# In the last but one attention slot, the last weight load is issued ahead of three row stores instead of behind them

## The chip, the cores and the metric

The kernel runs on one core of a Trainium2 chip. The metric is the device time of one execution in microseconds (us), as the median of several runs. The profile is one further execution of the same program, taken by the hardware profiler. All moments below are microseconds from the start of its span.

Five engines run their own instruction queues and meet at semaphores: TensorE (PE: matmuls; PEld is its weight load), VectorE (DVE), ScalarE (ACT), GpSimd (POOL) and SyncE (SP). SP and GpSimd issue the DMAs; the page of the profile shows SP's as queue q1 (hardware) and GpSimd's as queue q0 (software).

## The reference

Blockwise causal attention, and then a mixture of eight experts, of which each token uses one:

```python
# attention: batch 8, heads 8, sequence 576, head size 64; blocks of 64 positions
scores = where(block_of(q) >= block_of(k), q @ k.T / 8, -1e9)
x = softmax(scores) @ v                      # joined over heads: [8, 576, 512]

# experts: E = 8, D = 512, F = 1024, token after token within a batch
logits = x @ w_gate                          # [8, 576, 8]
local_gate = sigmoid(x @ w_local)
e = argmax(logits[s]) if s == 0 or local_gate[s] < 0.5 else previous e
p = softmax(logits[s])
out[s] = p[e] * (relu(x[s] @ w1[e]) @ w2[e])
```

The expert of a token can depend on all tokens before it in its batch.

## The kernel before, in words

**Attention.** A pair is two heads of one batch; the eight batches have four pairs each, 32 in all (`NPAIR`). A loop over `i` has one slot for each pair. Slot `i` issues the loads of q and k of pair `i + 2` (SP), the product of pair `i - 1` with its values (`values`, lines 998 and 1007), the scores of pair `i` (`scores`, lines 972 to 977), their exponentials on ScalarE, and the transposes of q and k of pair `i + 1` (`transposes`, tile `kq`, line 692). `add_chunks` (lines 1019 and 1021) adds up the chunks of a pair's exponentials on VectorE, for their sums.

**Rows of x.** In slots of their own, the finished pairs of a batch are transposed into token rows (`rows_of_batch`, PSUM tile `trx`), and VectorE multiplies them by the softmax's reciprocals into an SBUF tile (line 818). Up to batch 5 that tile is a slice of `xg`; for the later batches it is `x`, a tile of a pool with two buffers. Slot 30 makes three such tiles of batch 6: two in `x` and one, of 64 rows, in `xg`. Slot 31 makes two more, in the two buffers of `x` again. A call to `store` only notes the transfer to the DRAM tensor `x_rows`; `release` (line 677) issues what is noted, at the end of slots 0 to 30 on GpSimd's queue, and after slot 31 on SP's.

**Weights of the experts.** They lie in SBUF in bf16, `w1_bf` and `w2_bf` (both are called `w_bf` in the profile). `load_weights(e, layer)` is one DMA from GpSimd that converts 2 MB of f32 to 1 MB of bf16: line 107 for `w1`, line 111 for `w2`. There are sixteen, one in every second slot from slot 2 on for the first fourteen. The place of the last expert's `w1` holds routing scratch until slot 30, and that of its `w2` holds q and k that are waiting for their transposes, so these two loads come last: line 107 between the first gathers (`pending`), and line 111 at the end of slot 30.

**Experts.** Tokens are sorted into tiles of 128 by expert. `gather` (line 651, GpSimd) fetches a tile's rows from `x_rows` into `xg`; SP's DMA transpose turns it (line 1269 for the first four tiles, into a part of `S`; line 1393 for the others). `first_mm` (line 1093) multiplies by the tile's `w1`, which VectorE has copied out (line 1078 for tiles 0 and 1, into `Pc` and `qkT`; line 1297 for the others, `w1c`); ScalarE applies the relu (line 1096); `second_mm` (line 1335) multiplies by `w2_bf` in place, at an offset that is read at run time; ScalarE scales `y` (line 1340) and GpSimd scatters it to the output (line 1343). Tiles of the first five batches run while batch 7 is still being routed: its logits (lines 705 and 728), and `tokens` on VectorE with small products on TensorE between (lines 313 to 395).

**Order.** The scheduler is manual: each engine takes its instructions in the order in which the program is written, and semaphores for data and for buffers' reuse are put in by the framework. The transposes, the scores, the routing's products and `first_mm` of tile 0 all take PSUM from one pool of three buffers in rotation (tag `sc`). Between slot 31 and the later experts' tiles stands `nc.gpsimd.drain()` (line 1277).

Of the kernel before, what the change touches and what calls it, by code (L numbers as in the profile page):

```python
# [62 lines left out]
def kernel(  # L63
# [23 lines left out]
    E = moe_w_gate.shape[1]  # L87
# [17 lines left out]
    def load_weights(e, layer):  # L105
        if layer == 0:
            nc.gpsimd.dma_start(
                out=w1_bf[:, e * WE:(e + 1) * WE].rearrange("p (do f) -> p do f", f=F),
                in_=moe_w1[e].rearrange("(do di) f -> di do f", di=P))
        else:  # L110
            nc.gpsimd.dma_start(
                out=w2_bf[:, e * WE:(e + 1) * WE].rearrange("p (fo d) -> p fo d", d=Dm),
                in_=moe_w2[e].rearrange("(fo fi) d -> fi fo d", fi=P))

    HP = H // 2
    NPAIR = B * HP
# [715 lines left out]
    with tc.tile_pool(name="atn_const", bufs=1) as cst, \  # L832
# [24 lines left out]
        def load_qk(i):  # L857
            if i >= NPAIR:
                return
            b, p = divmod(i, HP)  # L860
            h2 = slice(2 * p, 2 * p + 2)
            tl = ld.tile([P, 2, D], F32, tag="qkl", name="qkl")
            raws[i] = [tl]
            for j, src in enumerate((k, q)):

                m = staged_of(i)[:, j].rearrange("p (h j d) -> p h j d", h=2, j=4)
                nc.sync.dma_start(
                    out=m.rearrange("p h j d -> p h (j d)"),
                    in_=src[b, h2, :512].rearrange("h (p j) d -> p h (j d)", j=4))
                raws[i].append(m)  # L870
            for j, src in enumerate((k, q)):
                nc.sync.dma_start(out=tl[64 * j:64 * j + 64],
                                  in_=src[b, h2, 512:].rearrange("h s d -> s h d"))
# [81 lines left out]
        def scores(i, u):  # L955
            if i >= NPAIR:
                return
            if u == 0:
                Ss[i] = Sb[i % NSB]
            t = qkTs[i % 2]  # L960
            ps = psp.tile([P, 2, 512], F32, tag="sc", name="sc")
            col = 0
            for c, q0, n in UNITS[u]:
                for half in (1, 0):
                    late = half
                    skip = ST if late and q0 == c * P else 0
                    k0 = c * P + ST * late
                    for h in range(2):
                        r = slice(64 * h, 64 * h + 64)
                        to = ps[64 * half:64 * half + 64, h]  # L970
                        if skip and c == 0:
                            nc.tensor.matmul(to[:, col:col + ST], lhsT=t[r, 0, LAST:],
                                             rhs=t[r, 1, LAST:], start=True, stop=True)
                        elif skip:
                            nc.tensor.matmul(to[:, col:col + ST], lhsT=minus[r], rhs=ones_b[r, :ST],
                                             start=True, stop=True)
                        nc.tensor.matmul(to[:, col + skip:col + n], lhsT=t[r, 0, k0:k0 + ST],  # L977
                                         rhs=t[r, 1, q0 + skip:q0 + n], start=True, stop=True)
                col += n
            return ps  # L980

        def exps(i, u, ps):
            if i >= NPAIR:
                return
            for col, n, c, q0 in EXPS[u]:
                rows = slice(0, P)
                nc.scalar.activation(exps_at(i, c, q0, n, rows), ps[rows, :, col:col + n],  # L987
                                     func=AF.Exp, scale=scale_attn)
# [88 lines left out]
        def weights_at(w, ev):  # L1077
            nc.vector.tensor_copy(w, w1_bf[:, bass.ds(ev, WE)])
            return w
# [21 lines left out]
        def expert(ph, j, engines=(mybir.EngineType.PE, mybir.EngineType.DVE)):  # L1101
            return nc.values_load(
                et_i[ph][0:1, j:j + 1], engines=engines, min_val=0,
                max_val=(E - 1) * WE,
                skip_runtime_bounds_check_because="the table is clamped to the last expert")

        def bf(x, n):
            return x.rearrange("p a s -> p (a s)").bitcast(BF16)[:, :n]
# [62 lines left out]
        def behind(i):  # L1171

            def between():
                if i % HP == 2 and i < NPAIR - 2 or i == NPAIR - HP or not routing(i) and i > 1:
                    vector(AHEAD_OF[i % HP])
                run(sums)
                if sums:
                    routing(i)

            sums = sums_of(i)  # L1180
            if sums:
                values(i - 1, between)
            else:
                values(i - 1)
                between()
            if not swap:
                add_chunks(i - 1)
            if i == NPAIR - 2:
                mask(i - 1, nc.vector)
            load_v(i + 1)  # L1190
            if i > 1 and not rows_first(i):
                vector(AFTER[i % HP])
# [5 lines left out]
        for i in range(NPAIR):  # L1198
            slot[0] = i
            load_qk(i + 2)  # L1200


            swap = i == 1
            if not swap:
                behind(i)
            if i == NPAIR - 1:

                tiles = [(0, j) for j in range(NS[0])] + [(1, j) for j in range(NS[1])]
                ev = {j: expert(*tiles[j]) for j in range(2)}
                w = weights_at(bf(Pc[0], WE), ev[0])  # L1210
            for u in range(len(UNITS)):
                ps = scores(i, u)
                if u < 2 or i < 2:
                    exps(i, u, ps)
                if u == 0:
                    if i == 0:
                        transposes(1, 8)
                        constants()
                        for h in range(2):
                            hs = slice(64 * h, 64 * h + 64)  # L1220
                            nc.sync.dma_start(
                                out=wg2[hs, :, 16 * h:16 * h + E],
                                in_=moe_w_gate.rearrange("(p h d) e -> h d p e", h=2, d=D)[h])
                            nc.sync.dma_start(
                                out=wg2[hs, :, 16 * h + E:16 * h + E + 1],
                                in_=moe_w_local.rearrange("(p h d) e -> h d p e", h=2, d=D)[h])
            if swap:
                behind(i)
            last = lambda: exps(i, 2, ps) if i > 1 else None
            if i == NPAIR - 2:  # L1230
                last()
                last = lambda: None
                run([lambda: half_batch(B - 1, 0)])
            if i:
                transposes(i + 1, 6 if swap else 0,
                           last)
            if swap:
                add_chunks(i - 1)
            if i == NPAIR - 1:
                routing(i)  # L1240
            run(turns_of(i))
            if rows_first(i):
                vector(AFTER[i % HP])
            slot[0] = i + 0.5
            if i % HP == 0 or NPAIR - 3 <= i < NPAIR - 1:
                routing(i)
            if i < NPAIR - 1:
                vector(END[i % HP])
            early_mask = i % 2 == 0 and i <= NPAIR // 2
            if early_mask:  # L1250
                mask(i - 1, nc.gpsimd)
            arrange(i + 2, [nc.gpsimd.tensor_copy] * 2)
            if not early_mask and i != NPAIR - 2:
                mask(i - 1, nc.gpsimd)
            while pending:
                pending.pop(0)()

            if wload < 2 * E - 2 and i == 2 + 2 * wload:
                load_weights(*divmod(wload, 2))
                wload += 1  # L1260
            if i < NPAIR - 1:
                release(queue=nc.gpsimd)
            if i == NPAIR - 2:

                free = bf(Sb[(NPAIR - 3) % NSB], 2 * S * 2)[:, -AHEAD * Dm:]
                xTs = {}
                for j in range(AHEAD):
                    xTs[j] = free[:, j * Dm:(j + 1) * Dm].rearrange("p (k n) -> p k n", k=KO1)
                    nc.sync.dma_start(out=xTs[j], in_=row_of_x(xgs[j]), transpose=True)
                load_weights(E - 1, 1)  # L1270
        assert not pending
        slot[0] = NPAIR
        release()
# [17 lines left out]
    with ExitStack() as ffn:  # L1291
# [184 lines left out]
        i = len(tiles) - 1  # L1476
# [37 lines left out]
```

## Time and profile before

| What | Value |
|---|---|
| Time, median of 3 runs | 408.97 us (408.6 to 411.11) |
| Time of the profiled execution | 408.54 us |
| Its span | 406.5 us |
| PE busy | 392.6 us |
| DVE, ACT, POOL busy | 242.2, 228.7, 196.1 us |
| Queue q0 (GpSimd's DMAs) | 34.84 MB, 41.6% of 16 engines' span |
| Queue q1 (SP's DMAs) | 34.19 MB, 37.2% |
| Loads of weights | 16, 1024 KB each, median 9.9 us from issue to landing |

A row of a timeline reads: start, duration, engine, line, operation, what is written `<-` what is read, shapes, count; in brackets the engine's idle time before it and what ended that. A row of the DMA view reads: transfer, issuing queue, count, size of one, and the median time from issue to landing, where the profile has it.

### The profile page before, as it was taken

How to read it: one execution, taken by the hardware profiler on the slowest of the kernel's cores; microseconds unless marked ns; L12 is line 12 of the kernel's file. 1: busy time of each engine (PE TensorE's matmuls, PEld its weight loads, DVE VectorE, ACT ScalarE, POOL GpSimd, SP SyncE). 2: the span in 40 equal slices, each digit the busy share in tenths (PEclk: the TensorE clock that was granted, in tenths of full speed). 3: DMA queues.
4: the chain of work that ended last, by engine and by line, in shares of the span. 5: the costliest groups of instructions: out<-in, count | busy, mean ns of one | idle time of the engine just before them, and what ended most of it. 6: DMA issues, size and time to landing. Idle time of an engine off the chain costs nothing. (4 is left out here: it accounts for less than half of the span.)

```text
span 406.5 us, 14547 instructions
## 1 busy us (share of the span) xinstructions
PE 392.6 (97%) x5834; PEld 285.5 (70%) x5834; DVE 242.2 (60%) x505; ACT 228.7 (56%) x391; POOL 196.1 (48%) x250
## 2 busy tenths in 40 slices
PE   9999999999999999999998998998999999999985
PEld 7667677677677677667766666666777777777763
DVE  2463564564564577967899975977887333333320
ACT  3758557567557557657647465333545555555542
POOL 1244251342341342582632363074776888888833
PEclk9999999999999999999999999999999999999999
DMA  6588989999999979999989689944763645655532
GB/s 178 142 190 194 216 172 222 201 201 228 194 202 210 183 183 246 174 202 244 170 192 237 136 155 192 151 109 120 166 168 97 170 135 148 154 149 149 128 99 78
DMA packets 108819, 69.97 MB, mean 172 GB/s; under 512 B 74847, under 2 KB 100255, under 8 KB 108752
## 3 DMA queue, kind: packets, MB, share of 16 engines
q0 software_dynamic: 19200, 34.84, 41.6%
q1 hardware_dynamic: 89552, 34.19, 37.2%
q8 instruction: 48, 0.79, 0.8%
q14 instruction: 19, 0.16, 0.1%
HBM read 66.88 MB, written 14.70 MB: 201 GB/s over the span
## 5 line engine op out<-in xcount | busy, mean ns | idle before, releaser
L1019 DVE TENSOR_TENSOR S<-S,Pc 128x896 f32<-128x896 f32 (+2 forms) x96 | 84.0, 875 | 23.9 <-PE o L998 19.1
L977 PE MATMUL sc<-qkT 64*64 64x224 f32 (+6 forms) x1536 | 91.6, 367 | 0.0
L1297 DVE COPY w1c<-w_bf 128x4096 bf16 x36 | 44.3, 1231 | 55.6 <-PE ps_h L1093 52.8
L1093 PEld LDWEIGHTS <-w1c 128*128 128x128 bf16 x1152 | 67.2, 98 | 9.1 <-issue 1.3
L880 POOL COPY w_bf<-w_bf 128x512 f32<-128x512 f32 x61 | 43.9, 737 | 60.8 <-DMA w_bf<-in_k_dram 33.0
L977 PEld LDWEIGHTS sc<-qkT 64*64 64x64 f32 x1536 | 70.5, 134 | 3.7 <-issue 2.5
L1335 PE MATMUL ps_y<-w_bf,hT 128*128 x296 | 69.9, 379 | 1.0 <-DMA w_bf<-in_moe_w_dram 1.0
L987 ACT ACTIVATE Pc<-sc 128x448 f32<-128x448 f32 (+1 forms) x96 | 68.1, 716 | 0.0
L1093 PE MATMUL ps_h<-xT,w1c 128*128 128x128 bf16 x1088 | 66.3, 219 | 1.3 <-ACTq L1474 1.1
L1343 POOL DMA_INDIRECT out_dram<-y,idx x37 | 56.2, 1519 | 22.0 <-ACT y L1340 12.2
L651 POOL DMA_INDIRECT xg<-x_rows,idx x38 | 47.1, 1239 | 31.3 <-issue 13.9
L1096 ACT ACTIVATE hT<-ps_h 128x512 bf16<-128x512 f32 x76 | 45.3, 597 | 26.2 <-PE ps_h L1093 24.6
L998 PE MATMUL o<-Pc,v 128*64 128x320 f32 (+2 forms) x512 | 57.3, 366 | 0.0
L998 PEld LDWEIGHTS o<-Pc,v 128*64 128x64 f32 x512 | 34.6, 137 | 24.1
L1340 ACT ACTIVATE y<-ps_y,xg 128x512 f32<-128x512 f32 x37 | 25.4, 687 | 45.5 <-PE ps_y L1335 39.1
L987 ACT ACTIVATE S<-sc 128x576 f32<-128x576 f32 x64 | 42.0, 656 | 12.6 <-PE sc L977 12.1
L1335 PEld LDWEIGHTS <-hT 128*128 128x128 bf16 x296 | 27.5, 98 | 27.3 <-issue 1.0
L1011 ACT COPY oT<-o 128x576 f32<-128x576 f32 x32 | 20.5, 641 | 35.7 <-PE o L1007 35.7
L1026 POOL MEMSET S<- 64x128 f32 x30 | 6.0, 200 | 69.8 <-DVE S L1021 40.7
L818 DVE TENSOR_TENSOR xg<-trx,rs 128x512 bf16<-128x512 f32 (+1 forms) x31 | 20.2, 685 | 25.9 <-PE trx L692 25.8
L998 PE MATMUL o<-S,v 128*64 128x192 f32 (+1 forms) x256 | 34.7, 392 | 0.3 <-ACT qkT L925 0.3
L714 ACT COPY LT<-trg 128x320 f32<-128x320 f32 x15 | 6.4, 426 | 44.4 <-PE trg L705 44.4
(313 smaller groups left out, 467.4 us busy)
## 6 DMA issues: line engine op xcount, KB each, us to landing
w_bf<-in_moe_w_dram POOLq DMA_DIRECT2D x16, 1024.0 KB, 9.9
w_bf<-in_k_dram SPq DMA_DIRECT2D x32, 256.0 KB, 3.4
w_bf<-in_q_dram SPq DMA_DIRECT2D x32, 256.0 KB, 7.7
v<-in_v_dram SPq DMA_DIRECT2D x64, 128.0 KB, 5.8
x_rows<-xg POOLq DMA_DIRECT2D x24, 128.0 KB, 8.1
qkl<-in_k_dram SPq DMA_DIRECT2D x32, 32.0 KB, 3.8
qkl<-in_q_dram SPq DMA_DIRECT2D x32, 32.0 KB, 5.7
vl<-in_v_dram SPq DMA_DIRECT2D x32, 32.0 KB, 7.4
```

Source lines behind the costliest of these rows:

```text
L651: st = nc.gpsimd.indirect_dma_start(out=x, out_offset=None, in_=x_dram[:rows], in_offset=bass.IndirectOffsetOnAxis(ap=row_of(ph, j), axis= ...
L880: copies[j](m, raws[i][1 + j].rearrange("p h j d -> p j h d"))
L977: nc.tensor.matmul(to[:, col + skip:col + n], lhsT=t[r, 0, k0:k0 + ST], rhs=t[r, 1, q0 + skip:q0 + n], start=True, stop=True)
L987: nc.scalar.activation(exps_at(i, c, q0, n, rows), ps[rows, :, col:col + n], func=AF.Exp, scale=scale_attn)
L998: nc.tensor.matmul(po[64 * h:64 * h + 64, VO + q0:VO + q0 + n], lhsT=vs[i][c][:, h, :], rhs=exps_at(i, c, q0, n, slice(0, P))[:, h, :], st ...
L1019: nc.vector.tensor_add(Ss[i][:, :, P * c:], Ss[i][:, :, P * c:], Pc[i % 2][:, :, POS[c]:POS[c] + n])
L1093: nc.tensor.matmul(ps[:, fo, :], lhsT=w[:, ko * F + f0:ko * F + f0 + P], rhs=xT[:, ko, :], start=(ko == 0), stop=(ko == KO1 - 1))
L1096: relu[0] = nc.scalar.activation(hT[:, half * (FO // 2):(half + 1) * (FO // 2), :], ps, func=AF.Relu)
L1297: ended["w"] = nc.vector.tensor_copy(w, w1_bf[:, bass.ds(ev[i], WE)])
L1335: nc.tensor.matmul(ps, lhsT=hT[:, fo, :], rhs=w2_bf[:, bass.ds(ev + fo * Dm, Dm)], start=(fo == 0), stop=(fo == FO - 1))
L1340: nc.scalar.activation(y, ps, func=AF.Copy, scale=factor)
L1343: st = nc.gpsimd.indirect_dma_start(out=out_flat, out_offset=bass.IndirectOffsetOnAxis(ap=row_of(ph, j), axis=0), in_=y, in_offset=None, b ...
```

## The change

In slot 30, the call that loads the last expert's `w2` stands ahead of `release(queue=nc.gpsimd)`, which issues the three noted stores, and no longer behind the block of DMA transposes that follows it. No work is added or removed.

```diff
@@ -1258,6 +1258,8 @@
             if wload < 2 * E - 2 and i == 2 + 2 * wload:
                 load_weights(*divmod(wload, 2))
                 wload += 1
+            if i == NPAIR - 2:
+                load_weights(E - 1, 1)
             if i < NPAIR - 1:
                 release(queue=nc.gpsimd)
             if i == NPAIR - 2:
@@ -1267,7 +1269,6 @@
                 for j in range(AHEAD):
                     xTs[j] = free[:, j * Dm:(j + 1) * Dm].rearrange("p (k n) -> p k n", k=KO1)
                     nc.sync.dma_start(out=xTs[j], in_=row_of_x(xgs[j]), transpose=True)
-                load_weights(E - 1, 1)
```

On GpSimd, at the end of slot 30, this moves one row (line 111 is the weight load, line 677 a store of rows, line 651 a gather, line 1026 a memset of slot 31):

```order
 L107 DMA w_bf<-in_moe_w_dram 128x4x1024
 L651 DMA xg<-x_rows,idx_89 128x257 x2
+L111 DMA w_bf<-in_moe_w_dram 128x8x512
 L677 DMA x_rows<-x 128x256 x2
 L677 DMA x_rows<-xg 64x256
-L111 DMA w_bf<-in_moe_w_dram 128x8x512
 L1026 MEMSET S 64x2x64
 L651 DMA xg<-x_rows,idx_89 128x257 x3
```

The weight load passes the three stores and nothing else; SP's transposes of line 1269 (1270 in the changed file) are on another queue, in the order that they had. GpSimd's DMAs take eight semaphores in turn, so that each store's semaphore is now the next one. On VectorE, in slot 31, the two instructions that write `x` again wait for the first two stores, before and now:

```order
 L355 TENSOR_TENSOR pay<-lt_g,valid 128x10 [waits DVE_49]
 L357 TENSOR_TENSOR oh<-w_78,pay 128x80 [waits DVE_49]
-L818 TENSOR_TENSOR x<-trx,rs 128x2x4x64 [waits DMASW3_49,PE_49]
-L818 TENSOR_TENSOR x<-trx,rs 128x2x4x64 [waits DMASW4_49]
+L818 TENSOR_TENSOR x<-trx,rs 128x2x4x64 [waits DMASW4_49,PE_49]
+L818 TENSOR_TENSOR x<-trx,rs 128x2x4x64 [waits DMASW5_49]
 L366 COPY lt_g<-rtr 128x80 [waits PE_49]
 L368 COPY ltmp_g<-rtr 128x80
```

The instructions of VectorE stand where they stood; only the numbers of the semaphores moved on by one, with the stores.

## The prediction

> **What bounds the kernel now.** I read the page first, then the stretches around the change, then the timelines of the engines that meet there. The page's first part and four stretches:
>
> ```profile
> PE 392.6 (97%) x5834; PEld 285.5 (70%) x5834; DVE 242.2 (60%) x505; ACT 228.7 (56%) x391; POOL 196.1 (48%) x250
> ```
> ```profile
> 250.00:256.00 6.00, 5.55 (x93) 4.43 (x95) 4.67 (x10) 3.36 (x7) 0.20 (x1) 1.00 1.30 186
> 256.00:262.00 6.00, 5.71 (x90) 4.34 (x86) 5.64 (x11) 2.82 (x6) 0.00 (x0) 1.00 1.28 177
> 262.00:264.00 2.00, 1.31 (x7) 0.69 (x8) 1.65 (x4) 0.52 (x2) 0.00 (x0) 1.00 0.42 118
> 276.00:389.00 113.00, 112.01 (x1284) 82.44 (x1285) 56.91 (x100) 58.27 (x93) 87.13 (x61) 1.00 0.55 142
> ```
>
> TensorE bounds the whole. The column before the last is the DMA share: from 250 to 262 the sixteen DMA engines are full (1.30, 1.28), after 262 they are not (0.42). From 276 to 389 PE is busy for 112.01 of 113 us: what is lost before 276 is not won back. TensorE around the change:
>
> ```profile
> 257.08 2.07 PE L1093 MATMUL ps_h<-S,Pc 128*128 128x128 bf16 x32
> 259.75 1.96 PE L1093 MATMUL ps_h<-S,qkT 128*128 128x128 bf16 x32
> 262.69 1.89 PE L1335 MATMUL ps_y<-w_bf,hT 128*128 x8 [0.97 <-DMA w_bf<-in_moe_w_dram]
> 264.51 1.28 PE L705 MATMUL trg<-S,sel 128*32 128x320 f32 x16
> 266.85 0.38 PE L728 MATMUL trl<-id_f,LTl 128*128 128x128 f32 x2
> 273.11 0.27 PE L330 MATMUL rta<-id_f,S 128*5 128x128 f32 x1 [0.80 <-DVE S L327]
> 276.15 0.19 PE L340 MATMUL rtb<-S,ones_f 5*5 5x5 f32 x2 [1.05 <-DVE S L337]
> ```
>
> Two things are seen. The first `second_mm` waits 0.97 us for a weight load; it reads `w2_bf` at a run-time offset, so it waits for every load, the last one included. And at 273 and 276 PE waits for DVE. GpSimd and DVE in the same stretch:
>
> ```profile
> 241.76 0.83 POOL L107 DMA_DIRECT2D w_bf<-in_moe_w_dram  x1
> 244.25 1.01 POOL L651 DMA_INDIRECT xg<-x_rows,idx  x1 [0.31 <-issue]
> 246.66 1.16 POOL L677 DMA_DIRECT2D x_rows<-x  x2 [1.40 <-DVE x L818]
> 247.84 0.54 POOL L677 DMA_DIRECT2D x_rows<-xg  x1
> 248.38 0.93 POOL L111 DMA_DIRECT2D w_bf<-in_moe_w_dram  x1
> 264.15 1.14 POOL L651 DMA_INDIRECT xg<-x_rows,idx  x1 [10.58 <-issue]
> ```
> ```profile
> 255.93 0.24 DVE L357 TENSOR_TENSOR oh<-w,pay 128x80 bf16<-128x80 f32 x1
> 256.09 1.28 DVE L818 TENSOR_TENSOR x<-trx,rs 128x512 bf16<-128x512 f32 x2
> 257.58 1.22 DVE L1078 COPY qkT<-w_bf 128x4096 bf16 x1
> 258.72 2.60 DVE L1019 TENSOR_TENSOR S<-S,Pc 128x896 f32<-128x896 f32 x3
> 264.73 0.30 DVE L382 TENSOR_TENSOR lt_g<-lt_g,ltmp_g 128x80 f32<-128x80 f32 x1
> 265.93 0.49 DVE L710 TENSOR_TENSOR LTl<-LTl,trg 128x320 f32<-128x320 f32 x1 [0.91 <-PE trg L705]
> ```
>
> L818 at 256.09 overwrites the two `x` buffers that the stores of 246.66 read, so it waits for their landing; here it follows L357 without a gap.
>
> **What the load wins.** It waits for the transposes of pair 31, which read its place in SBUF:
>
> ```profile
> 244.47 0.67 PE L692 MATMUL kq<-id_f,w_bf 64*128 64x64 f32 x16
> ```
>
> They end at 245.14, and the gather of 244.25 leaves GpSimd at 245.26. So the load is issued at about 245.3 instead of 248.38, and its 0.93 us end at 246.2, before the stores, which wait for DVE until 246.66 as now. GpSimd's own time costs nothing: the 0.93 us fit into the 1.40 that it idles there, and without that idle time the stores would be issued 0.93 later. At most the 0.97 us of PE go away.
>
> **What the stores lose.** Their packets now stand behind 1 MB on q0. Transfers of GpSimd, each with its issue and its landing, first the pairs in which a store already follows a weight load in the program of before, then a store with none ahead, then the gather and the first store of slot 30:
>
> ```profile
> 55.13 0.75 POOL L107 DMA_DIRECT2D w_bf<-in_moe_w_dram  x1
> 55.91 1.15 POOL L677 DMA_DIRECT2D x_rows<-xg  x2
> 85.43 0.81 POOL L107 DMA_DIRECT2D w_bf<-in_moe_w_dram  x1
> 86.29 1.14 POOL L677 DMA_DIRECT2D x_rows<-xg  x2
> 125.65 0.54 POOL L677 DMA_DIRECT2D x_rows<-xg  x1 [4.47 <-DVE xg L818]
> ```
> ```profile
> w_bf<-in_moe_w_dram POOLq DMA_DIRECT2D x1, 1024.0 KB, 9.8
> x_rows<-xg POOLq DMA_DIRECT2D x1, 128.0 KB, 11.0
> w_bf<-in_moe_w_dram POOLq DMA_DIRECT2D x1, 1024.0 KB, 11.5
> x_rows<-xg POOLq DMA_DIRECT2D x1, 128.0 KB, 11.0
> x_rows<-xg POOLq DMA_DIRECT2D x1, 128.0 KB, 5.2
> xg<-x_rows,idx POOLq DMA_INDIRECT x1, 7.9
> x_rows<-x POOLq DMA_DIRECT2D x1, 128.0 KB, 8.5
> ```
>
> At 55 the weights land at 55.13 + 9.8 = 64.9 and the store behind them at 55.91 + 11.0 = 66.9, 2.0 later; at 85 they land at 96.9 and 97.3, 0.4 later. With no load ahead a store takes 5.2. The queue serves in the order of issue. In slot 30 too: gather 244.25 + 7.9 = 252.15, first store 246.66 + 8.5 = 255.16, and the weights at about 262.65, where PE stops waiting, 7.5 us after that store.
>
> Now the weights come right behind the gather: 252.15 + 7.5 = 259.65. The first store lands 0.4 to 2.0 later, from 260.0 to 261.65. Another upper bound is the queue's end: the bytes are the same and the engines are full until 262, so the last of the three stores lands at about 262.6 and the first not later. I take 261.6: at 55, as here, the load has a store of 128 KB and a second one behind it on a full machine, and here a third follows.
>
> [...]
>
> **The sum.** L818 moves from 256.09 to 261.6, by 5.5 us, and everything behind it on DVE with it, since DVE takes its queue in order: the copy of tile 1's weights (257.58), the chunks of S (258.72), and the routing up to L382 (ends 265.03, now 270.5).
>
> - By PE. The three PSUM buffers go in rotation to the routing's `rtd`, to `trx` (which L818 reads), to the routing's `rtr`, and then to the two halves of tile 0's `first_mm`: so the second half, halfway through the row of 257.08, at about 258.1, needs L818's buffer. L818 ends at 257.37 + 5.5 = 262.87, and PE stalls there for 4.8. Tile 1 needs the copy (ends 258.80 + 5.5 = 264.3) and starts at 259.75 + 4.8 = 264.55: no more lost. `second_mm` of tile 0 then finds its weights there, which takes 0.97 off: PE is 3.85 late.
> - By DVE. L710 had 0.91 of idle time before it, waiting for PE. It comes 5.5 - 0.9 = 4.6 late, more than PE. PE needs its result at 266.85, and the waits for DVE at 273.11 and 276.15 show that DVE ends last there. So PE leaves this stretch 4.6 late.
>
> From 276 on PE has no idle time to absorb it. The drain on GpSimd (10.58 idle until 264.15) I take to end with the queue, about where it did; if it came some us later, that would be covered by tiles 2 and 3, whose rows are in SBUF, since the tiles that those gathers feed come after 276. Sum: 408.54 + 4.6 = 413.1 us, against the profiled execution's own time, of which 2.0 us lie around its span of 406.5; it is 0.4 under the median of 408.97. With the landing at 260.0 the shift is 3.9 and the sum 408.54 + 3.0 = 411.5; with 262.6 it is 6.5, and 414.1.
>
> **The rivals.**
>
> 1. *Stores are late, but counted from their issue.* If 11.0 us from issue to landing is the price whatever is queued before, the first store lands at 246.66 + 11.0 = 257.7. The shift is 1.6, less 0.9: 409.2. Against it: the 8.5 us without a load in front already contain the wait for the load of 241.76, which the rows of 55 and 85 don't have.
> 2. *Stores slip past the weights, and the change is a gain.* Then L818 stays at 256.09, PE saves 0.97, and DVE's idle 0.91 shrinks as PE's work comes sooner: 408.54 - 0.9 = 407.6. It decides at a landing before 256.1. For it: the interval between the two landings at 85 is only 0.4, and the store is an eighth of the load. Against it: in no pair quoted does the store come first. [...]
> 3. *More than the buffers is late.* SP's transposes for tiles 0 and 1 share the engines with 1 MB instead of the stores; if tile 0's comes later than 257.08, or the stores land behind the queue's end at 262.6, each us adds itself: 414.1 to 415.
>
> **How the numbers follow.** A measurement of this kernel can tell about 1% (4.1 us) from no change. The forecast (411.5 to 414.1) has 0.74, rival 1 has 0.12, rival 2 0.07, rival 3 0.07. The range from 409.2 to 414.6 takes in the forecast, rival 1 and the near half of rival 3. The edge of 1% is 413.06, just under my number: of the forecast's 0.74 I put 0.46 above it, which with rival 3 makes 0.53 for slower. Rival 2 misses the 1% too, so almost all the rest is "same".
>
> **What will show it.** In the changed profile L111 is issued at about 245.3 and the stores still at 246.66; DVE's L818 has a wait of some 5 us that a DMA `x_rows<-x` ends, and starts at about 261.6; PE waits for DVE inside tile 0's `first_mm`; the wait for the weights at the first L1335 is gone; PE's rows from 276 on are the same, about 4.6 later. It is wrong if the stores land before 256.1, if L818 isn't the instruction that waits, or if a later stretch of PE loses less than it does at 273.

## The result, and the profile after

| Program | Median | Runs | Lowest to highest | Ratio to before, 95% interval |
|---|---|---|---|---|
| before | 408.79 us | 6 | 407.75 to 411.11 | |
| changed | 414.76 us | 6 | 410.81 to 419.85 | 1.0111 [1.0064, 1.0159] |

The change costs time: about 1.1%. (The ratio leaves out two of the six executions, 417.49 and 419.85, which lie more than 1.5% above the fastest, so it is smaller than the ratio of the medians; the profile of one experiment, e7, is of such a slow execution.) The profiled execution took 412.42 us, 3.88 more than that of before; its span is 410.4 us, 3.9 longer. The forecast was 413.1.

The page's first part, and then windows of TensorE's granted clock (`PEclk`, the column before the last two) and of the DMA engines (the column after it):

```profile
PE 392.6 (96%) x5834; PEld 287.0 (70%) x5834; DVE 245.0 (60%) x505; ACT 228.6 (56%) x391; POOL 194.4 (47%) x250
```
```profile
256.00:262.00 6.00, 1.80 (x32) 1.52 (x31) 1.80 (x6) 1.24 (x2) 0.00 (x0) 0.95 0.87 184
262.00:264.00 2.00, 2.00 (x19) 1.48 (x20) 2.00 (x2) 0.41 (x1) 1.09 (x1) 0.50 0.22 70
264.00:276.00 12.00, 12.00 (x146) 8.38 (x138) 9.89 (x32) 4.97 (x9) 4.62 (x4) 0.97 0.39 78
276.95:389.00 112.05, 110.84 (x1263) 81.18 (x1264) 58.30 (x103) 56.88 (x92) 84.49 (x60) 1.00 0.59 143
```

PE does the same work in the same busy time. From 256 to 262 it is busy for 1.80 us, where it was busy for 5.71 before: that is where the time goes. Then something stands there that the program of before doesn't show at all: a granted clock of 0.50 from 262 to 264. GpSimd, with the gather, the load and the stores:

```profile
244.10 1.00 POOL L651 DMA_INDIRECT xg<-x_rows,idx  x1 [0.31 <-issue]
245.28 0.94 POOL L111 DMA_DIRECT2D w_bf<-in_moe_w_dram  x1 [0.18 <-issue]
246.50 1.14 POOL L677 DMA_DIRECT2D x_rows<-x  x2 [0.28 <-DVE x L818]
...
262.90 1.09 POOL L651 DMA_INDIRECT xg<-x_rows,idx  x1 [9.49 <-issue]
```

The load is issued at 245.28 and the stores follow at 246.50. VectorE, which overwrites the stores' buffers:

```profile
255.78 0.24 DVE L357 TENSOR_TENSOR oh<-w,pay 128x80 bf16<-128x80 f32 x1
259.86 0.69 DVE L818 TENSOR_TENSOR x<-trx,rs 128x512 bf16<-128x512 f32 x1 [3.84 <-DMA x_rows<-x]
260.91 0.69 DVE L818 TENSOR_TENSOR x<-trx,rs 128x512 bf16<-128x512 f32 x1 [0.36 <-DMA x_rows<-x]
...
269.79 0.49 DVE L710 TENSOR_TENSOR LTl<-LTl,trg 128x320 f32<-128x320 f32 x1 [0.54 <-PE trg L705]
```

The first L818 waits 3.84 us until the first store has landed, and the second another 0.36 for the second store. And TensorE:

```profile
256.40 1.06 PE L1093 MATMUL ps_h<-S,Pc 128*128 128x128 bf16 x16
261.66 1.89 PE L1093 MATMUL ps_h<-S,Pc 128*128 128x128 bf16 x16 [4.20 <-DVE x L818]
263.48 1.30 PE L705 MATMUL rtr<-oT,wg 128*32 128x320 f32 x8
264.71 2.00 PE L1093 MATMUL ps_h<-S,qkT 128*128 128x128 bf16 x32
266.55 1.89 PE L1336 MATMUL ps_y<-w_bf,hT 128*128 x8
...
270.71 0.38 PE L728 MATMUL trl<-id_f,LTl 128*128 128x128 f32 x2
...
276.95 0.27 PE L330 MATMUL rta<-id_f,S 128*5 128x128 f32 x1 [0.79 <-DVE S L327]
```

Between the two halves of tile 0's `first_mm` PE waits 4.20 us for L818. The second half then takes 1.89 us for the sixteen products that take 1.06 in the first half: that is the clock of 0.50. The wait for the weights at the first L1336 is gone. At 276.95 PE starts on the routing of batch 7 (`rta`), 3.84 later than before (273.11), and keeps that to the end: from there to the end of the span it is 133.4 us in both (406.5 - 273.11 and 410.4 - 276.95).

**A measure for what follows.** The executions differ by some us already where this stage begins (L357 starts at 253.82 to 256.96 in the table below), and not always in the direction of the change. So the profiles are compared by one stretch, from the start of L357 (255.93 before, 255.78 after) to the start of `rta` (273.11 and 276.95): 17.18 us before, 21.17 after. The difference, 3.99, is the whole of the change in this execution.

### The profile page after: what moved, and what is told of

Same layout as the page of the kernel before. It is cut to its first block, busy times and chain, and to the rows that moved or that the text cites. A ratio compares the mean times of both kernels' runs of the same rounds, so it can differ in the third digit from the quotient of the medians.

```text
span 410.4 us, 14547 instructions
## 1 busy us (share of the span) xinstructions
PE 392.6 (96%) x5834; PEld 287.0 (70%) x5834; DVE 245.0 (60%) x505; ACT 228.6 (56%) x391; POOL 194.4 (47%) x250
## 5 line engine op out<-in xcount | busy, mean ns | idle before, releaser
L1019 DVE TENSOR_TENSOR S<-S,Pc 128x896 f32<-128x896 f32 (+2 forms) x96 | 85.5, 891 | 21.7 <-PE o L998 16.9
L977 PE MATMUL sc<-qkT 64*64 64x224 f32 (+6 forms) x1536 | 90.3, 364 | 0.0
L880 POOL COPY w_bf<-w_bf 128x512 f32<-128x512 f32 x61 | 42.7, 715 | 77.2 <-DMA w_bf<-in_k_dram 33.8
L1093 PEld LDWEIGHTS <-w1c 128*128 128x128 bf16 x1152 | 67.2, 98 | 9.1 <-DVE w1c L1298 0.9
L1336 PE MATMUL ps_y<-w_bf,hT 128*128 x296 | 69.9, 379 | 0.0
L1093 PE MATMUL ps_h<-xT,w1c 128*128 128x128 bf16 x1088 | 66.3, 219 | 1.2 <-ACTq L1475 1.1
L1344 POOL DMA_INDIRECT out_dram<-y,idx x37 | 55.2, 1491 | 22.0 <-issue 9.8
L998 PEld LDWEIGHTS o<-Pc,v 128*64 128x64 f32 x512 | 36.2, 137 | 22.7
L1336 PEld LDWEIGHTS <-hT 128*128 128x128 bf16 x296 | 27.5, 98 | 26.2
L818 DVE TENSOR_TENSOR xg<-trx,rs 128x512 bf16<-128x512 f32 (+1 forms) x31 | 20.2, 685 | 25.4 <-PE trx L692 25.2
```

The source lines that it names most:

```text
L880: copies[j](m, raws[i][1 + j].rearrange("p h j d -> p j h d"))
L998: nc.tensor.matmul(po[64 * h:64 * h + 64, VO + q0:VO + q0 + n], lhsT=vs[i][c][:, h, :], rhs=exps_at(i, c, q0, n, slice(0, P))[:, h, :], st ...
L1019: nc.vector.tensor_add(Ss[i][:, :, P * c:], Ss[i][:, :, P * c:], Pc[i % 2][:, :, POS[c]:POS[c] + n])
L1093: nc.tensor.matmul(ps[:, fo, :], lhsT=w[:, ko * F + f0:ko * F + f0 + P], rhs=xT[:, ko, :], start=(ko == 0), stop=(ko == KO1 - 1))
L1336: nc.tensor.matmul(ps, lhsT=hT[:, fo, :], rhs=w2_bf[:, bass.ds(ev + fo * Dm, Dm)], start=(fo == 0), stop=(fo == FO - 1))
L1344: st = nc.gpsimd.indirect_dma_start(out=out_flat, out_offset=bass.IndirectOffsetOnAxis(ap=row_of(ph, j), axis=0), in_=y, in_offset=None, b ...
```

## The experiments

Two theories were to be told apart. The first, that of the prediction: the stores land late because they stand behind 1 MB, and only the reuse of the two `x` buffers by L818 makes that cost anything. The rival: the earlier load itself costs, by its place in the DMA engines or through another waiter, and the buffers' wait only shows where that surfaces. The edits are to the changed program unless said otherwise. All profiles in one table (a_again, e1, e2 and e5 ran on one chip, e3, e4 and e6 on a second, and the last three on a third, on which the program of before took 413.1 us; medians are of all runs):

| Program | Median | Ratio to before, 95% | L357 | `rta` | Stretch |
|---|---|---|---|---|---|
| before | 408.79 | | 255.93 | 273.11 | 17.18 |
| changed | 414.76 | 1.0111 [1.0064, 1.0159] | 255.78 | 276.95 | 21.17 |
| a_again: changed, repeated | 412.72 | 1.0106 [1.0066, 1.0147] | 256.96 | 279.20 | 22.24 |
| e1: changed, no reuse of `x` | 407.24 | 0.9936 [0.9901, 0.9972] | 255.52 | 271.75 | 16.23 |
| e2: before, no reuse of `x` | 407.55 | 0.9975 [0.9933, 1.0018] | 253.82 | 271.12 | 17.30 |
| e3: load between the stores | 408.32 | 1.0001 [0.9965, 1.0037] | 254.72 | 272.68 | 17.96 |
| e4: stores on SP's queue | 414.07 | 1.0147 [1.0089, 1.0205] | 255.35 | 277.45 | 22.10 |
| e5: half of the load ahead | 409.93 | 0.9995 [0.9954, 1.0035] | 256.33 | 274.21 | 17.88 |
| e6: products in PE's gap | 415.41 | 1.0188 [1.0126, 1.0251] | 256.24 | 277.30 | 21.06 |
| e7: stores on ScalarE's queue | 417.08 | 0.9969 [0.9898, 1.004] | 255.11 | 274.85 | 19.74 |
| e1 repeated | 413.05 | 0.9993 [0.9953, 1.0033] | 254.87 | 272.96 | 18.09 |
| e2 repeated | 412.65 | 1.001 [0.9972, 1.0049] | 256.85 | 273.33 | 16.48 |

Three programs were profiled twice: the changed one (21.17 and 22.24), e1 (16.23 and 18.09) and e2 (17.30 and 16.48). So the stretch of one and the same program varies by 0.8 to 1.9 us, and a smaller difference between two programs isn't established by it; the 4 to 5 us of the change lie well beyond that.

**The change repeated (a_again).** Only a comment differs.

> The changed kernel itself, timed again beside the others. [...] If the first profile was an accident of that execution (rival: the landing varies by more than it costs), L818 starts within 1 us of 256 in this one and the time is within 1 us of the kernel before.

Measured: 1.0106 [1.0066, 1.0147], twelve runs. L818 starts at 261.32, not within 1 us of 256. The same two waits, the second one longer (VectorE, then TensorE):

```profile
261.32 0.69 DVE L818 TENSOR_TENSOR x<-trx,rs 128x512 bf16<-128x512 f32 x1 [4.11 <-DMA x_rows<-x]
263.28 0.69 DVE L818 TENSOR_TENSOR x<-trx,rs 128x512 bf16<-128x512 f32 x1 [1.27 <-DMA x_rows<-x]
```
```profile
264.03 1.89 PE L1093 MATMUL ps_h<-S,Pc 128*128 128x128 bf16 x16 [5.40 <-DVE x L818]
```

The loss of 1.1% is there again, and so are the half clock (0.50 from 264 to 266) and the length of 1.89.

**No reuse of the buffers (e1, and e2 in the program of before).** The two tiles that slot 31 makes get places of their own, in SBUF that is free by then, instead of the two `x` buffers. The same edit in both programs:

```diff
                 x = (xgs[t][:, :XH] if b < NB1 + 1 or (b < B - 1 and t == AHEAD)
+                     else qkT.rearrange("p j a s -> p (j a s)")[:, 4 * S - XH:] if (b, t) == (B - 2, 2)
+                     else xgs[NX - 1][:, :XH] if (b, t) == (B - 2, 3)
                      else op.tile([P, XH], F32, tag="x", name="x"))
```

> The changed order, but the two row tiles of slot 31 get places of their own (the free tail of qkT and the sixth slice of xg), so that L818 has nothing to wait for. Theory (the loss is L818's wait for the stores that stand behind the weights): no wait at L818, no gap of PE in tile 0, the wait of 0.97 us for the weights gone as well: 407 to 408 us, 0.5 to 1.5 under the kernel before. Rival (the loss comes from the transfers themselves, for instance from the transposes for tiles 0 and 1 that now run beside 1 MB): the time stays at 411 to 413 us, with PE waiting for a DMA S<-xg.

> The order of before with the same two places of their own: what the other buffers alone do. Theory: in the kernel before L818 did not wait, so nothing changes, 408.5 to 409.2 us, and the wait of about 1 us for the last weights stays. Rival (the buffers help by themselves, so that the run with both changes says nothing of the order): 407.5 us or less.

In e1, VectorE and TensorE (L818 is L820 here, and L1336 is L1338):

```profile
255.68 0.68 DVE L820 TENSOR_TENSOR qkT<-trx,rs 128x512 bf16<-128x512 f32 x1
256.28 0.68 DVE L820 TENSOR_TENSOR xg<-trx,rs 128x512 bf16<-128x512 f32 x1
```
```profile
256.13 1.95 PE L1095 MATMUL ps_h<-S,Pc 128*128 128x128 bf16 x32
258.02 0.75 PE L705 MATMUL rtr<-oT,wg 128*32 128x320 f32 x8
258.77 1.95 PE L1095 MATMUL ps_h<-S,qkT 128*128 128x128 bf16 x32
260.55 1.89 PE L1338 MATMUL ps_y<-w_bf,hT 128*128 x8
```

And TensorE in e2, where the load stands behind the stores:

```profile
260.70 1.89 PE L1337 MATMUL ps_y<-w_bf,hT 128*128 x8 [0.62 <-DMA w_bf<-in_moe_w_dram]
```

With the load ahead of the stores exactly as in the change, but without the reuse, VectorE and PE don't wait, and the loss is gone: the stretch is 16.23 in place of 21.17, and the time 0.9936 of before. So the buffers' reuse is not where another loss surfaces, it is the loss. In e2 the edit alone changes nothing that can be measured: its 407.55 us lie under the 408.5 of the theory and just over the 407.5 of the rival, but its interval reaches over 1.

Whether the early load then wins something is another question. Here e1's stretch is 1.07 shorter than e2's, and e2 has a wait of 0.62 for the weights that e1 hasn't. Both were run once more as they were, on another chip:

> The changed order with places of their own for slot 31's two row tiles once more, beside the order of before with the same places. Theory: the load's own gain, 0.9 to 1.0 us, is the difference between the two: a stretch of 16.2 to 16.4 us, and a time 0.5 to 1.5 us under the kernel before. Rival (the order has no gain left, another wait takes its place): a stretch of 17 us or more, and the same time as the other.

> The order of before with places of their own for slot 31's two row tiles, once more. Theory: these places alone change nothing, since L818 did not wait there: a stretch of 17.1 to 17.4 us with the wait of PE for the last weights in it, and the time of the kernel before within 0.5 us. Rival (the places help by themselves): a stretch under 16.8 us, or 1 us or more off the time of the kernel before.

There the ratios were 0.9993 and 1.001, and the stretch was 18.09 with the load ahead and 16.48 with it behind. Both stretches went the way of their rivals, and both theories missed. So a gain of the load's own isn't established: on the first chip e1 took 0.6% less than before and e2 0.25% less, on the other neither did. As a version that beats both, e1 isn't confirmed either.

**Half of the load ahead (e5).** The load is split into two of 512 KB, one on each side of the stores.

```diff
             if i == NPAIR - 2:
-                load_weights(E - 1, 1)
+                load_half(0)
             if i < NPAIR - 1:
                 release(queue=nc.gpsimd)
             if i == NPAIR - 2:
+                load_half(1)
```

> The last weight load in two halves of 512 KB, one ahead of the three stores and one behind. Theory (the landing of the stores moves in proportion to what stands ahead of them on the queue): with 1 MB ahead the first store landed where L818 started, 259.9, with none at 255.2, so with 0.5 MB at about 257.5; L818 waits 1.5 to 2 us, PE stalls about 1 us and keeps its full clock, the weights are there when PE asks: 408.5 to 409.5 us. Rival (any load ahead costs its latency, whatever its size): L818 still starts at 259 or later, and the time is 411 or more.

VectorE, TensorE and a window with the clock (lines are seven further on: L825 is L818, L1100 is L1093):

```profile
258.19 1.29 DVE L825 TENSOR_TENSOR x<-trx,rs 128x512 bf16<-128x512 f32 x2 [1.61 <-DMA x_rows<-x]
```
```profile
259.53 1.07 PE L1100 MATMUL ps_h<-S,Pc 128*128 128x128 bf16 x16 [1.76 <-DVE x L825]
```
```profile
258.00:261.00 3.00, 1.47 (x24) 1.05 (x24) 2.81 (x6) 0.77 (x2) 0.00 (x0) 1.00 1.24 208
```

The wait shrinks from 3.84 + 0.36 to 1.61, and PE's gap from 4.20 to 1.76; the sixteen products behind the gap take 1.07 us, and the clock stays at 1.00. So the stores' lateness grew with the bytes ahead, and half the bytes cost 0.70 in the stretch, where all of them cost 3.99. (The 0.70 alone is within the spread of the stretch; the waits carry the reading.) The time can't be told from before.

**The load between the stores (e3).** The two stores from `x` go first, then the load, then the third store, whose tile nobody waits for here.

```diff
             if i == NPAIR - 2:
+                release(2, queue=nc.gpsimd)
                 load_weights(E - 1, 1)
```

> The weights between the second and the third store: the two stores that L818 waits for keep their place on the queue, and only the one of 64 rows, for which nobody waits but a gather behind the drain, stands behind the weights. Theory: L818 starts as in the kernel before, the weights land about 0.5 us sooner at most, 408.5 to 409.5 us against a kernel before of 408.8 to 409.6. Rival (moving the load up is harmful by itself): 411 us or more.

GpSimd, VectorE and TensorE:

```profile
245.45 1.15 POOL L677 DMA_DIRECT2D x_rows<-x  x2 [1.41 <-DVE x L818]
246.59 0.92 POOL L111 DMA_DIRECT2D w_bf<-in_moe_w_dram  x1
247.49 0.56 POOL L677 DMA_DIRECT2D x_rows<-xg  x1
```
```profile
254.88 1.28 DVE L818 TENSOR_TENSOR x<-trx,rs 128x512 bf16<-128x512 f32 x2
```
```profile
258.37 0.66 PE L1093 MATMUL ps_h<-S,Pc 128*128 128x128 bf16 x9 [0.50 <-issue]
...
262.22 1.89 PE L1337 MATMUL ps_y<-w_bf,hT 128*128 x8 [0.62 <-issue]
```

L818 doesn't wait, and the loss is gone with only two stores of 128 KB moved back ahead. The load passes one store of 64 KB here, and that buys nothing: the ratio is 1.0001, and PE still idles for 0.62 at L1337. The stretch is 17.96, 0.78 more than before, which is within its spread; 0.50 of idle time stand inside tile 0's `first_mm`, with no releaser that the profile shows.

**The stores on another queue (e4 and e7).** In e4 the three stores are issued by SP, behind the second of its DMA transposes; in e7 by ScalarE, where they stood.

```diff
             if i == NPAIR - 2:
                 load_weights(E - 1, 1)
-            if i < NPAIR - 1:
+            if i < NPAIR - 2:
                 release(queue=nc.gpsimd)
...
                     nc.sync.dma_start(out=xTs[j], in_=row_of_x(xgs[j]), transpose=True)
+                    if j == 1:
+                        release()
```
```diff
             if i < NPAIR - 1:
-                release(queue=nc.gpsimd)
+                release(queue=nc.scalar if i == NPAIR - 2 else nc.gpsimd)
```

> The changed order, but slot 30's three stores are issued by SP (hardware queue q1) behind the first two of the four transposes, so that the 1 MB of weights is on another queue than they are. Theory (the stores are late because they stand behind the weights on GpSimd's one queue): they land before about 256, L818 waits less than 1 us, PE has no gap of over 1 us in tile 0, and the time is 407 to 409 us. Rival (the sixteen engines are full whatever the queue, and a store beside 1 MB of weights lands as late as one behind it): L818 starts at 259 or later and the time is 411 or more.

> The changed order, with slot 30's three stores issued by ScalarE, whose queue holds no other DMA. On SP's queue they had landed late too, but there two slow transposes stood ahead of them, so that run did not separate queue from engines. Theory (a transfer is late by what stands ahead of it on its own queue): nothing stands ahead, the first store lands within 6 us of its issue, before 253, L818 does not wait, the weights' wait is gone: 407 to 408.5 us, a stretch from L357 to the routing's first product of 16.2 to 17.2 us. Rival (the engines are full, and any small transfer beside 1 MB of weights lands when that does): L818 starts over 3 us behind L357, the stretch is 20 us or more, and the time 411 or more.

SP's queue, VectorE and TensorE in e4:

```profile
243.38 2.86 SPq L1271 DMA_TRANSPOSE S<-xg  x2
246.34 1.68 SPq L677 DMA_DIRECT2D x_rows<-x  x2
```
```profile
258.75 0.69 DVE L818 TENSOR_TENSOR x<-trx,rs 128x512 bf16<-128x512 f32 x1 [3.15 <-DMA x_rows<-x]
260.65 0.69 DVE L818 TENSOR_TENSOR x<-trx,rs 128x512 bf16<-128x512 f32 x1 [1.21 <-DMA x_rows<-x]
```
```profile
261.40 1.89 PE L1093 MATMUL ps_h<-S,Pc 128*128 128x128 bf16 x16 [4.35 <-DVE x L818]
```

In e4 the stores are issued at 246.34, as early as in the change, on a queue without the load, and still L818 waits 3.15 + 1.21. That speaks against the first theory as it stood: 1 MB ahead on the same queue is not needed for late stores. They stood behind two transposes there, and whether those alone held them, or the full engines too (the two queues together took 112.9% of the sixteen engines' time from 244 to 253), e4 can't tell. ScalarE's queue has nothing ahead of them. In e7, GpSimd's queue, ScalarE's and VectorE:

```profile
244.62 0.94 POOL L111 DMA_DIRECT2D w_bf<-in_moe_w_dram  x1 [0.89 <-PE trx L692]
```
```profile
245.24 1.04 ACTq L677 DMA_DIRECT2D x_rows<-x  x2
```
```profile
256.48 0.69 DVE L818 TENSOR_TENSOR x<-trx,rs 128x512 bf16<-128x512 f32 x1 [1.12 <-DMA x_rows<-x]
257.70 0.69 DVE L818 TENSOR_TENSOR x<-trx,rs 128x512 bf16<-128x512 f32 x1 [0.53 <-DMA x_rows<-x]
```

Ratio and stretch of e7 are not used; the waits, which DMAs end, are. On a queue of their own, 0.6 us behind the load's issue at 244.62, the stores still take 11.2 us (245.24 to 256.48). L818 waits 1.12 + 0.53 in place of 3.84 + 0.36, but that shrinks also because the stores are issued sooner against L357 here. Counted from their issue, the first store took 8.5 us in before, 13.36 in the change (246.50 to 259.86) and 11.24 here: a queue of their own takes away 2.1 of the 4.9 us that the load had added, and 2.7 stay, which the load costs the stores as a neighbour on full engines (GpSimd's queue alone took 111.7% of their time from 244 to 247), or which the other chip adds; that isn't told apart. Both expectations missed: the store didn't land within 6 us, and L818 started 1.37 behind L357, not over 3.

**PE kept busy in the gap (e6).** Twelve products of zeros between the two halves of tile 0's `first_mm`, to see what the half clock costs.

```diff
+        left_out = [12]
+
+        def warm():
+            for _ in range(left_out.pop() if left_out else 0):
+                nc.tensor.matmul(po[:, :P], lhsT=zeros, rhs=zeros, start=True, stop=True)
...
-                        lambda: psp.tile([P, FO // 2, P], F32, tag="sc", name="ps_h"))
+                        lambda: psp.tile([P, FO // 2, P], F32, tag="sc", name="ps_h"), warm)
```

> The changed kernel with twelve products of zeros, whose result nobody reads, between the two halves of tile 0's first_mm, so that PE has work in most of its gap. Theory (a part of the loss, 0.4 to 0.6 us, is the half clock that follows the gap): no half clock there, the second half of tile 0 takes 1.0 to 1.1 us instead of 1.9, the stretch from the start of L357 to the first product of batch 7's routing is 0.4 to 0.6 us shorter for the same start of the second L818, and the time is 411.5 to 412.5 us, a difference that the times alone hardly show. Rival (the clock costs nothing, since DVE ends last anyway): the stretch is the same for the same start of L818.

TensorE, and a window behind the gap:

```profile
257.74 2.90 PE L1291 MATMUL o<-const-float32-0.0 128*128 128x128 f32 x24
262.34 1.07 PE L1093 MATMUL ps_h<-S,Pc 128*128 128x128 bf16 x16 [1.70 <-DVE x L818]
263.33 0.75 PE L705 MATMUL rtr<-oT,wg 128*32 128x320 f32 x8
```
```profile
262.00:264.00 2.00, 1.66 (x24) 1.05 (x24) 2.00 (x5) 0.56 (x1) 0.44 (x1) 1.00 0.37 131
```

The row of zeros counts 24 records for the twelve products. The clock stays at 1.00, and the two rows behind the gap take 1.07 and 0.75 in place of 1.89 and 1.30: 1.37 us less on PE. But the stretch is 21.06, hardly below 21.17, since L818 waited 4.45 here and 0.28 more went between L710 and `rta` (7.44 in place of 7.16, why is open); and the time, 415.41, is not lower than that of the change; the expectation missed. In the profile the half clock's price is therefore what PE adds over VectorE (next section), about half a us; in the times it can't be seen, and why this kernel's six runs came out 2.7 us above its own profiled 412.71 stays open.

## Why the prediction was right, and where it was off

**The load and the queue.** Issue of the load: forecast 245.3, measured 245.28; the stores 246.66 and 246.50. That the store lands behind the load is shown by the repeat, whose DMA view has the landings of the gather (issued at 245.30), the load (246.47) and the first store (247.69):

```profile
xg<-x_rows,idx POOLq DMA_INDIRECT x1, 7.5
w_bf<-in_moe_w_dram POOLq DMA_DIRECT2D x1, 1024.0 KB, 13.9
x_rows<-x POOLq DMA_DIRECT2D x1, 128.0 KB, 13.5
```

They land at 252.8, 260.4 and 261.2, in the order of issue. That the lateness comes from the load is shown by the series of first landings, read where L818's wait ends, from L357's start: no wait with none of the load ahead (before and e3), 1.86 us with half of it (258.19 - 256.33), 4.08 with all of it (259.86 - 255.78). That excludes rival 2 (no wait), and rival 1 too: it had L818 at 257.7 against 259.86. That the place on one queue is all of it, as the prediction had it, isn't shown: e4 and e7 had late stores on other queues, 11.2 us behind their issue in e7 with nothing ahead.

**The step that was off: the landing of the first store.** I took 261.6, from 252.15 for the gather, 7.5 for the weights and 1.95 for the store behind them. Measured is 259.86, just under the lower end of 260.0. The gather in front, issued at 244.10, took 7.1 us in this execution:

```profile
xg<-x_rows,idx POOLq DMA_INDIRECT x1, 7.1
```

It landed at 251.2, 0.95 earlier than in before, and the store 8.7 behind it instead of 9.45. So the load and the store together took 0.8 less than I took from the rows of 55, while the end at 85 (0.4 behind the weights, 7.9 in all) would have been 0.8 too little: the measured store lies between the two pairs. The repeat shows which of the two terms it was: the weights land 7.6 behind the gather, as forecast (7.5), and the store 0.8 behind the weights, not 1.95. So the term that was too large is the store behind the load, for which I took the 2.0 of 55 rather than the 0.4 of 85. My other bound, the queue's end at 262.6, was loose, because the engines are not full until 262 any more: 0.87 of them from 256 to 262, where it was 1.28.

**A term that I had not counted: the second store.** I moved L818's two instructions as one row. Each waits for its own store, and the second one waited 0.36 more (1.27 in the repeat, 1.21 in e4).

**VectorE's shift.** The pair of L818 ends at 261.60, 5.82 behind L357's start, where before it ended at 257.37, 1.44 behind it: a shift of 4.38, forecast 5.5. Less the idle 0.91 before L710, which the prediction named: 3.47 by VectorE, forecast 4.6.

**Which engine ends last.** Here the prediction was wrong. It had VectorE last and PE at 3.85. In the profile L710 waits 0.54 us for PE. PE's `second_mm` starts 10.77 behind L357's start, before 6.76: 4.01 late. Into that go the half clock's 0.83 (1.89 against 1.06) and some 0.55 (1.30 against the 0.75 of e6), 1.38 in all; without them PE would be 2.63 late and VectorE last, as forecast. So the clock adds about 0.5, and 3.47 + 0.54 is the measured 3.99 within the rounding. e6 bears that out: without the half clock L710 follows L382 with no wait for PE, though the pair of L818 ends later there (6.04 behind L357's start):

```profile
269.86 0.48 DVE L710 TENSOR_TENSOR LTl<-LTl,trg 128x320 f32<-128x320 f32 x1
```

What it didn't show is a shorter stretch, because of the longer wait at L818 and the 0.28 behind L710. The repeat goes by the same sum: the pair of L818 ends at 263.97, 7.01 behind L357's start, L710 waits 0.41 for PE, and 7.01 - 1.44 - 0.91 + 0.41 = 5.07, where its stretch is 5.06 longer than before.

**PE's wait through the PSUM buffer** was right: a stall inside tile 0's `first_mm`, forecast 4.8, measured 4.20, ended by L818. The weights' wait of 0.97 is gone, as forecast, and is worth nothing, since the other losses end later. Tile 0's first half starts at 256.40 without a wait, so SP's transposes were not late: rival 3 is excluded.

**Nothing is won back after 276**: 133.4 us remain in both. The drain on GpSimd ends 1.25 earlier, and no one sees it.

**The sum.** 3.9 us of span, forecast 4.6: the landing gave 1.1 less on VectorE, the clock 0.5 more. That 413.1 came so near to 412.42 is in part luck: the first L818 shifted by 3.9 (259.86 - 255.78 - 0.16) where I had 5.5, and two losses that I had not counted, 0.36 for the second store and about 0.5 for the clock, made up for half of that. The loss of 1.11% (1.06% in the repeat) lies at the edge of 1%, as the chances had it; both intervals reach over that edge on both sides.

## What to carry to other kernels

A large transfer that is moved ahead of small ones can make them late: here 1 MB ahead on the same queue took the first store from 8.5 to 13.4 us after its issue, and other queues helped only in part (12.4 us on SP's in e4, 11.2 on ScalarE's in e7). So ask who waits for the small ones, and above all who overwrites the buffers that they read, not only who waits for the large one. Here 0.97 us of waiting for a load was exchanged for 4.2 of waiting for a buffer, and giving the next writer another place, or leaving just those two stores ahead, took the loss away. And count what follows a stall on TensorE too: behind the 4.20 us here its granted clock was 0.50 from 262 to 264, and sixteen products took 1.89 us instead of 1.06.

## What the runs showed of the hardware

**The clock after a gap.** A gap of 4.20, 4.35 or 5.40 us on PE (changed, e4, a_again) was each time followed by sixteen products that took 1.89 us; behind gaps of 1.76 (e5) and 1.70 (e6) they took 1.07. Counted as half clock (twice the missing share of the clock, times the length of the window), the windows of the changed program give 0.6 us before 262, 2.0 up to 264 and 0.7 after it, some 3.3 in all. In e7 the gap was 1.70 us too, and yet the sixteen products behind it took 1.65, and the rows after them 1.30 and 2.37, which took 0.75 and 1.95 in e6; the page of e7 has a granted clock of 0.8 in its slice from 258.4 to 268.8.

```profile
258.45 1.65 PE L1093 MATMUL ps_h<-S,Pc 128*128 128x128 bf16 x16 [1.70 <-DVE x L818]
```

So these six gaps don't show that the length alone decides it, and what else might is not shown.

**A queue of its own was not a free path.** On ScalarE's queue in e7, with nothing ahead, a store of 128 KB took 11.2 us beside the load, though 5.2 were enough at 125 in the program of before. How much of that is the load's doing and how much the other chip's is not shown.

**The chips differed by about as much as this change costs.** The program of before had medians of 408.79, 409.64 and 408.8 us beside the result and the first seven experiments, and 413.1 beside the last three, on another chip. There the part behind `rta` took 139.2 us (e1 repeated: its span of 412.2 less 272.96) instead of 133.4. What makes it longer is not shown.
